# Adding partial sums in DRAM by the storing transfer, and letting ScalarE empty the accumulators

## The chip, the cores and the metric

The kernel runs on one core of a Trainium2 chip. The metric is device time in microseconds of one execution of the program. The median of three runs of the kernel before is 725.49 us (725.46 to 725.61).

## The reference

Attention over a small memory, then a gated feed-forward layer, all in float32, for 8 batches of 8 heads, 576 positions, head width 64:

```python
a = softmax(phi, over positions)                  # phi: (8, 8, 576, 32)
k_m, v_m = a^T k, a^T v                           # 32 memory rows per head
attn = softmax(q k_m^T / 8) v_m                   # (8, 8, 576, 64)
x = attn with heads side by side                  # (4608, 512)
out = (sigmoid(x w_gate) * (x w_val)) w_out       # d_ff = 1536
```

The output has 4608 rows of 512; each batch owns 576 of them.

## The kernel before

The hidden width of 1536 is cut into 12 tiles of 128, called f (0 to 11). A *step* is one batch with one f: TensorE makes gate and value (tiles `pu_t`) in two column halves c = 0 and 1 (`gate_half`), ScalarE takes the sigmoid (`sg`), VectorE the product, and the product is split in a high and a low part (`g_hi`, `g_lo`); then `out_half` multiplies it with the output weights into four accumulators in PSUM, `acc0` to `acc3`, one per 128 rows (t = 0 to 3) of the batch. Columns past 512 of two batches are gathered in `left` and done apart (`out_left`).

Batches 4 to 7 go through all 12 f at once. Batches 0 to 3 go in three rounds of four f (`turns`, L839): round one does f 0 to 3 for batches 0, 1, 2, 3, round two f 4 to 7, round three f 8 to 11. After each round a batch's accumulators have to leave, since the next batch uses the same four. That makes 48 steps, numbered 0 to 47; the first 12 are written out by hand (`OPENING`), the rest run in the loop at L1187, and after it (from L1352) batches 4 to 7 follow with an order of every engine written out by hand (`step`, `queued`: each instruction stands behind the last one of its engine).

In the loop, `out_half` lags: a finished f's half c = 0 is multiplied in the next step and its half c = 1 at the beginning of the one after (`pend`, `LAG` = 3). So for the last f of a round, tiles 0 and 1 leave in the step after and tiles 2 and 3 one step later. The next batch writes `acc0` and `acc1` again about one step after they left, and `acc2` and `acc3` likewise. The order of all TensorE instructions is that of the code (`in_turn`, L183). A scheduler orders the other engines' instructions of the loop; it follows the code's order where it can.

How a tile leaves is `leave` (L727). In round one it copies the accumulator into a tile called `row` (128 x 512; ScalarE for odd t, VectorE for even t), and GpSimd stores it into a DRAM tile `part`. In rounds two and three the earlier sum has been loaded from `part` into a `row` beforehand (`row_of`, L754, on SyncE's queue), VectorE adds accumulator and `row` (L732), and GpSimd stores the sum to a new `part` (round two) or to the output (round three). The loads are asked for one f ahead of the end (L722 to L725, and L1207 to L1209 for the last batch).

There are four rooms for `row` (`bufs=4`). A tile that asks for one waits until the transfer that read its last holder has landed. The rooms are also used by others: in steps 32 to 37 (L1197 to L1206) each step takes two of them for differences of the gate weights, made by VectorE at L1205 and stored by SyncE to the kept weights (`wgv`); late on, the left columns of batches 2 to 7 (`left_hi`, `left_lo`, L769) and the memories of batches 6 and 7 (L379, L413) take them.

Transfers are issued by `move` (L169) on two queues: "batch" is SyncE (SP), "stream" is GpSimd (POOL). On each, the transfers start in the order of the code. POOL has the stores of `row`, and in steps 12 to 30 the loads of weight words that are converted there. SP has everything else: loads of `row`, reloads of `at`, kept weights, inputs of the next batches. A transfer that reads what another one wrote waits for that one's landing, and the queue waits with it.

Of the kernel before, what the change touches and what calls it, by code (L numbers as in the profile page):

```python
# [9 lines left out]
F32 = mybir.dt.float32  # L10
# [3 lines left out]
ALU = mybir.AluOpType  # L14
# [3 lines left out]
P = 128  # L18
B, H, S, D, M = 8, 8, 576, 64, 32
DM, DFF = 512, 1536  # L20
NG = 2
NKT = 4
NFT = DFF // P
SF = 4
# [14 lines left out]
QUAD = 4  # L39
TURN = 4  # L40
# [58 lines left out]
def attn_moe_kernel(  # L99
# [10 lines left out]
    nc = tc.nc  # L110

    keep = ctx.enter_context(tc.tile_pool(name="keep", bufs=1))
    dram = ctx.enter_context(tc.tile_pool(name="dram", bufs=1, space=bass.MemoryType.DRAM))
    sb = ctx.enter_context(tc.tile_pool(name="att", bufs=1))
    mb = ctx.enter_context(tc.tile_pool(name="moe", bufs=1))
    early = ctx.enter_context(ExitStack())
    po = ctx.enter_context(tc.tile_pool(name="po", bufs=1, space=PSUM))
    banks = ctx.enter_context(ExitStack())
    pu = banks.enter_context(tc.tile_pool(name="pu", bufs=NB, space=PSUM))
    pools = {"conv": early.enter_context(tc.tile_pool(name="conv0", bufs=1))}  # L120
# [14 lines left out]
    def att(shape, name, bufs=1):  # L135
        return sb.tile(shape, F32, name=name, bufs=bufs)
# [11 lines left out]
    def wo_of(f):  # L148
        return [t[:, f % NE, :] for t in wos[f // NE]]
# [16 lines left out]
    queues = {"batch": nc.sync, "stream": nc.gpsimd}  # L166
    last_move = {}

    def move(dst, src, queue="batch"):  # L169


        with ExitStack() as behind:
            if queue in last_move:
                behind.enter_context(tc.issue_after(last_move[queue].ins))
            last_move[queue] = queues[queue].dma_start(dst, src)  # L175

    def rest(lo, x, hi):

# [12 lines left out]
    def matmul(*args, **kw):  # L191
        in_turn(nc.tensor.matmul, *args, **kw)
# [109 lines left out]
    def convert(f, k):  # L302
        to_f32(whole_of(f, k), f, k)
        if k == 2:
            wo_hi(f)
            wo_lo(f)
# [257 lines left out]
    def again(b):  # L564
        new_at(b)
        for d, a in zip(kept[b], at[b]):
            move(a.rearrange("p r n -> p (r n)").bitcast(F32), d)
# [4 lines left out]
    def make_u(b, fs):  # L572

        nf = len(fs)
        pb = [bank()[:, : nf * 256].rearrange("p (f x) -> p f x", f=nf) for _ in range(2)]
        for p in range(H):
            rs, l = of_head(b, 1, p)
            js = slice((p // 2) * M, (p // 2 + 1) * M)
            r = wg[rs, fs[0] : fs[0] + nf, ORDER[b % 2][p] // 2, :]
            matmul(pb[p % 2][js], l, r, start=True, stop=True)  # L580
        U[b, fs[0], "pb"] = pb
# [21 lines left out]
    def part_u(b, fs):  # L603
        for r in range(2):
            u_hi(b, r, *fs)
            u_lo(b, r, *fs)
# [12 lines left out]
    @contextmanager  # L619
    def behind():  # L620


        with ExitStack() as stack:
            for last in (last_act, last_prod, last_u, last_conv):
                stack.enter_context(tc.issue_after(last[0].ins))
            yield
# [3 lines left out]
    part = {}  # L630
# [68 lines left out]
    def gate_all(b, f, c):  # L699
        for do in (gate_half, sigmoid, product, g_hi, g_left, g_lo):  # L700
            do(b, f, c)

    def out_half(b, f, c, at_start, at_end, later=False):

        hi, lo = G.pop((b, f, c))
        w_hi, w_lo = wo_of(f)
        if lo is None:
            terms = [(hi, raws[f])]
        else:
            terms = [(hi, w_hi), (hi, w_lo), (lo, w_hi)]  # L710
        for j in range(2):
            t = 2 * c + j
            if at_start:
                acc[b, t] = po.tile([P, DM], F32, name=f"acc{t}")
            ts = slice(j * P, (j + 1) * P)
            for i, (l, r) in enumerate(terms):
                last = at_end and i == len(terms) - 1
                matmul(acc[b, t], l[:, ts], r, start=at_start and i == 0, stop=last)
        if at_end and not later:
            for j in range(2):  # L720
                leave(b, f, 2 * c + j)
        if (b, f + 1) in ends and c:  # L722
            for t in range(SF):
                if (b, t) in part and (b, t) not in rows:
                    rows[b, t] = row_of(b, t)  # L725

    def leave(b, f, t):  # L727

        o = acc.pop((b, t))
        st = last_rows(t) if b == B - 1 else rows.pop((b, t), None) or row_of(b, t)  # L730
        if (b, t) in part:
            nc.vector.tensor_tensor(st, o, st, op=ALU.add)  # L732
            part.pop((b, t))
        elif t % 2 or "banks" in pools:
            nc.scalar.copy(st, o)
        else:
            nc.vector.tensor_copy(st, o)
        if f == NFT - 1:
            queue = "batch" if b >= QUAD else "stream"
            move(out[b * S + t * P : b * S + (t + 1) * P, :], st, queue)  # L740
        else:
            part[b, t] = dram.tile([P, DM], F32, name=f"part{b}_{t}_{f}")
            move(part[b, t], st, "stream")

    rows = {}
    room_of_last = []

    def last_rows(t):

        if not room_of_last:  # L750
            room_of_last.append(att([P, SF, 512], "kvm0"))
        return room_of_last[0][:, t, :]

    def row_of(b, t):  # L754

        st = mb.tile([P, DM], F32, name="row", bufs=4)
        if (b, t) in part:
            move(st, part[b, t])
        return st

    def u_tiles():
        return [mb.tile([P, 2, 2, 256], F32R, name=f"u_{p}", bufs=2) for p in ("hi", "lo")]
# [41 lines left out]
    def run(*parts):  # L804
        for p in parts:
            for _ in p:
                pass
# [34 lines left out]
    ends = {(b, f) for b, f, _, at_end in steps if at_end}  # L842
# [157 lines left out]
    MAIN = begin[QUAD, 0]  # L1000
# [28 lines left out]
    def go_on():  # L1029

        nonlocal pieces, slots
        for _ in range(-(-pieces // max(slots, 1))):
            next(beside, None)
            pieces -= 1
        slots -= 1
# [8 lines left out]
    def load_pair(n):  # L1044

        if n >= NPAIRS:
            return
        in_ring[n] = lp[0].tile([P, 2, NKT, 256], F32, name="ring")
        move(in_ring[n].rearrange("p f k n -> p (f k n)"), kept_w[n % NP])
# [137 lines left out]
    for i, (b, f, at_start, at_end) in enumerate(steps[:MAIN]):  # L1187
        if i < LISTED:
            continue
        if i in sides:  # L1190
            run(beside)
            beside, pieces = chain(*(g for _, g in sides[i])), sum(n for n, _ in sides[i])
            length = next(n for n in range(i + 1, len(steps) + 1) if n == len(steps) or steps[n][2]) - i
            slots = 2 * length - 1 - sum(i <= n < i + length for n in quad_at)
        if i in returns:
            again(returns[i])
        k = i - begin[0, NFT - TURN]  # L1197
        if 0 <= k < NP:
            w, kept_k = wg[:, 2 * k : 2 * k + 2], kept_w[k].rearrange("p (f k n) -> p f k n", f=2, k=NKT)
            move(kept_k[D:], w[D:])  # L1200
            move(kept_k[:D, :, :, :P], w[:D, :, :, :P])
            for j in range(2):
                t = mb.tile([P, DM], F32, name="row", bufs=4)[:D]
                t = t.rearrange("p (k n) -> p k n", k=NKT)
                nc.vector.tensor_tensor(t, w[:D, j, :, :P], w[:D, j, :, P:], op=ALU.subtract)  # L1205
                move(kept_k[:D, j, :, P:], t)  # L1206
        if i == MAIN - 2:  # L1207
            for t in range(SF):
                rows[b, t] = row_of(b, t)  # L1209
        if i == MAIN - TURN:  # L1210
            weights.close()
            lp[0] = weights.enter_context(tc.tile_pool(name="late2", bufs=1, side="right", reuse_waits="tile"))
            load_pair(0)
        extra = out_left(*lefts[i]) if i in lefts else iter(())
        gate_all(b, f, 0)
        for job in CONVERT.get(i, ()):
            with behind():
                convert(*job)
        next(extra, None)
        if i in u_at:  # L1220
            if steps[i + 1][0] != b:
                run(beside)
            make_u(*u_at[i])
            part_u(*u_at[i])
        while len(pend) >= LAG:
            out_half(*pend.pop(0))
        pend.append((b, f, 0, at_start, at_end))
        go_on()
        gate_all(b, f, 1)
        while len(pend) >= LAG and i < MAIN - 1:  # L1230
            out_half(*pend.pop(0))
        if i in quad_at:
            quad(i)
        if i == MAIN - 2:
            pair_u(0, [bank(), bank()])
            for name in "rl":
                u_out(0, name)
            u_sums(0, 0, 1, 2)
            for name in "lrs":
                part_hi(0, name)  # L1240
                part_lo(0, name)
        pend.append((b, f, 1, at_start, at_end))
        next(extra, None)
        if i not in quad_at:
            go_on()
        del U[b, f]
# [283 lines left out]
```

## Time and profile before

| | |
|---|---|
| median of three runs | 725.49 us |
| the profiled execution | 725.69 us, its span 723.9 us |
| PE (TensorE) | busy 98% of the span |
| DVE (VectorE) | 74% |
| ACT (ScalarE) | 58% |
| POOL (GpSimd) | 5% |
| DMA | 124.64 MB, 172 GB/s in the mean |

PE is TensorE's matmul, PEld its weight load, SP is SyncE with its queue SPq. L189 is the line of the helper that records every matmul, L175 that of the helper that issues every transfer, so rows are told apart by their tiles. "Time to landing" of a transfer runs from its issue to its landing. The rounds lie as follows: round one ends at about 165 us, round two at about 270, round three at about 389; steps 36 to 38, the first three of batch 1 in the third round, run from about 287 to 306 us, six microseconds each.

### The profile page before, as it was taken

To read this page: it belongs to the slowest core of one execution; us is meant where nothing else is said; L and a number is where in the kernel's file an instruction comes from. 1 tells how busy PE (TensorE), PEld (TensorE's weight loads), DVE (VectorE), ACT (ScalarE), POOL (GpSimd) and SP (SyncE) were. 2 spreads that over 40 slices of the span, in tenths; PEclk is the share of its full clock that TensorE was granted. 3 is DMA by queue.
4 is the path that set the end of the run, shared out by engine and by line. 5 is a ranking of instruction groups with operands and counts; after the bars stand their busy time and mean duration, and the time that the engine had idled before them with its cause. 6 is when DMAs were issued, how large, how long until landed. Compare 5 with 4: busy or idle time off the path is not lost.

```text
span 723.9 us, 14181 instructions
## 1 busy us (share of the span) xinstructions
PE 710.5 (98%) x5524; PEld 583.4 (81%) x5524; DVE 535.6 (74%) x1048; ACT 423.0 (58%) x984; POOL 36.3 (5%) x71
## 2 busy tenths in 40 slices
PE   8899999999999999999999999999999999999997
PEld 6656778888888988988878877887788788888786
DVE  5999998767777855567549678776787768977663
ACT  4676775454444433336455676875777657686553
POOL 0000100111102110110101000000000000000000
PEclk9999999999999999999999999999999999999999
DMA  8994629649457549871557113652323422141102
GB/s 349 420 389 141 253 83 379 238 137 363 136 191 264 175 158 225 305 247 33 160 216 275 59 59 114 226 182 68 109 73 114 146 94 78 59 175 60 59 1 73
DMA packets 37907, 124.64 MB, mean 172 GB/s; under 512 B 4241, under 2 KB 11665, under 8 KB 31697
## 3 DMA queue, kind: packets, MB, share of 16 engines
q1 hardware_dynamic: 31744, 103.04, 40.3%
q0 software_dynamic: 6096, 20.71, 8.1%
q8 instruction: 43, 0.70, 0.4%
q14 instruction: 24, 0.19, 0.1%
HBM read 94.90 MB, written 28.84 MB: 171 GB/s over the span
## 4 chain that ended last, share of the span: by engine, by line
PE 87%; DVE 6%; ACT 3%; DMA 2%; issue 1%; SPq 0%; DVEq 0%; ACTq 0%
PE acc L189 36%; PE pu_t L189 25%; PE c L189 8%; PE a L189 8%; PE b L189 5%; PE d L189 5%; DMA kvm<-in_kvm_dram 2%; ACT ph L164 1%; DVE e L484 1%; DVE e L501 1%; DVE zs L497 1%; DVE mx L482 1%; DVE e L475 1%; DMA q<-in_qT_dram 0%; SPq L175 0%
## 5 line engine op out<-in xcount | busy, mean ns | idle before, releaser
L189 PE MATMUL pu_t<-at,u_hi 128*128 128x320 f32 (+1 forms) x752 | 156.2, 303 | 0.2 <-DVE sg L672 0.2
L189 PE MATMUL acc<-wo_hi,g_hi 128*128 128x512 f32 x372 | 151.2, 406 | 0.0
L189 PE MATMUL acc<-wo_hi,g_lo 128*128 128x512 f32 x372 | 146.8, 395 | 0.0
L189 PE MATMUL acc<-wo_lo,g_hi 128*128 128x512 f32 x372 | 146.5, 394 | 0.0
L189 PEld LDWEIGHTS pu_t<-at,u_hi 128*128 128x128 f32 x752 | 124.2, 188 | 11.8 <-issue 3.0
L189 PE MATMUL pu_t<-at,u_lo 128*128 128x320 f32 (+1 forms) x360 | 106.3, 295 | 0.0
L189 PEld LDWEIGHTS acc<-wo_hi,g_hi 128*128 128x128 f32 x372 | 69.8, 188 | 34.2 <-issue 11.7
L189 PEld LDWEIGHTS acc<-wo_hi,g_lo 128*128 128x128 f32 x372 | 69.9, 188 | 17.1 <-DVE g_lo L179 0.8
L164 ACT ACTIVATE sg<-pu_t 128x256 f32<-128x256 f32 (+1 forms) x94 | 38.6, 411 | 75.8 <-PE pu_t L189 75.7
L189 PEld LDWEIGHTS acc<-wo_lo,g_hi 128*128 128x128 f32 x372 | 70.0, 188 | 6.3
L672 DVE TENSOR_TENSOR sg<-pu_t,sg 128x256 f32<-128x256 f32 (+1 forms) x92 | 41.5, 454 | 42.8 <-ACT sg L164 29.9
L682 ACT CAST g_hi<-sg 128x256 fp32r<-128x256 f32 x90 | 36.4, 406 | 54.5 <-DVE sg L672 53.3
L189 PEld LDWEIGHTS pu_t<-at,u_lo 128*128 128x128 f32 x360 | 67.8, 188 | 0.0
L1155 ACT COPY c_p<-c 128x288 f32<-128x288 f32 x48 | 19.2, 400 | 53.3 <-PE c L189 52.8
L179 DVE TENSOR_TENSOR g_lo<-sg,g_hi 128x256 fp32r<-128x256 f32 x90 | 37.4, 419 | 11.0 <-ACT g_hi L682 11.0
L1159 DVE TENSOR_TENSOR z<-c,c_x 128x288 f32<-128x288 f32 x48 | 21.9, 456 | 31.8 <-PE c L189 28.6
L164 ACT ACTIVATE z<-z 128x288 f32<-128x288 f32 x96 | 37.9, 438 | 7.5 <-DVE z L1159 7.4
L1171 ACT CAST g_hi<-z 128x512 fp32r<-128x512 f32 x48 | 29.9, 622 | 17.7 <-DVE z L1166 17.7
L1159 DVE TENSOR_TENSOR z<-a,c_s 128x288 f32<-128x288 f32 x48 | 21.7, 452 | 24.4 <-PE a L189 22.8
L179 DVE TENSOR_TENSOR u_lo<-pu_t,u_hi 128x512 fp32r<-128x512 f32 (+1 forms) x46 | 28.6, 672 | 10.5 <-ACT u_hi L595 10.5
L179 DVE TENSOR_TENSOR g_lo<-z,g_hi 128x512 fp32r<-128x512 f32 x48 | 32.8, 683 | 1.2 <-ACT g_hi L1171 1.2
L595 ACT CAST u_hi<-pu_t 128x512 fp32r<-128x512 f32 (+1 forms) x46 | 24.0, 587 | 13.8 <-PE pu_t L189 13.6
(246 smaller groups left out, 1473.1 us busy)
## 6 DMA issues: line engine op xcount, KB each, us to landing
ring<-wgv SPq DMA_DIRECT2D x24, 1024.0 KB, 4.8
at<-at SPq DMA_DIRECT2D x24, 576.0 KB, 6.8
kvm<-in_kvm_dram SPq DMA_DIRECT2D x12, 1024.0 KB, 10.2
q<-in_qT_dram SPq DMA_DIRECT2D x16, 512.0 KB, 4.7
part<-row POOLq DMA_DIRECT2D x32, 256.0 KB, 4.9
row<-part SPq DMA_DIRECT2D x32, 256.0 KB, 4.0
wg<-in_kvm_dram SPq DMA_DIRECT2D x4, 1024.0 KB, 11.8
out_dram<-row POOLq DMA_DIRECT2D x16, 256.0 KB, 5.1
```

The lines of the kernel that those rows point to most:

```text
L164: last_act[0] = nc.scalar.activation(*args, **kw)
L179: return nc.vector.tensor_tensor(lo, x, hi.bitcast(F32), op=ALU.subtract)
L189: last_pe[0] = do(*args, **kw)
L475: nc.vector.transpose(blocks(b, c)[:, r].rearrange("p w m -> p (w m)"), t)
L482: nc.vector.tensor_reduce(mx, e, axis=AX.X, op=ALU.max)
L484: nc.vector.tensor_tensor(e, e, mx.unsqueeze(3).broadcast_to([P, 2, w, M]), op=ALU.subtract)
L595: nc.scalar.copy(hi[:, r, :nf], U[b, fs[0], "pb"][r])
L672: last_prod[0] = nc.vector.tensor_tensor(prod, ps[1][:, :n], sg[:, :n], op=ALU.mult)
L682: nc.scalar.copy(hi, prod[:, : 2 * P])
L1155: nc.scalar.copy(getattr(self, name), self.c if name == "p5" else self.d)
L1159: nc.vector.tensor_tensor(self.z[:, i], x, y, op=ALU.add)
L1171: nc.scalar.copy(self.g[0], self.z[:, 2:4, : 2 * P])
```

## The change

In rounds two and three nothing is loaded any more. ScalarE copies the accumulator into a `row` for all four tiles (before, VectorE added there), and GpSimd's storing transfer adds it in DRAM to the batch's `part` (`accum_op=ALU.add`). There is one `part` per tile for all three rounds. In the third round GpSimd then issues a second transfer that copies the finished `part` from DRAM to the output. A `row` is asked for when the tile leaves. Round one and batches 4 to 7 are as before.

```diff
--- before.py
+++ after.py
@@ -166,13 +166,13 @@
     queues = {"batch": nc.sync, "stream": nc.gpsimd}
     last_move = {}
 
-    def move(dst, src, queue="batch"):
+    def move(dst, src, queue="batch", **kw):
 
 
         with ExitStack() as behind:
             if queue in last_move:
                 behind.enter_context(tc.issue_after(last_move[queue].ins))
-            last_move[queue] = queues[queue].dma_start(dst, src)
+            last_move[queue] = queues[queue].dma_start(dst, src, **kw)
 
     def rest(lo, x, hi):
 
@@ -719,30 +719,26 @@
         if at_end and not later:
             for j in range(2):
                 leave(b, f, 2 * c + j)
-        if (b, f + 1) in ends and c:
-            for t in range(SF):
-                if (b, t) in part and (b, t) not in rows:
-                    rows[b, t] = row_of(b, t)
 
     def leave(b, f, t):
 
         o = acc.pop((b, t))
-        st = last_rows(t) if b == B - 1 else rows.pop((b, t), None) or row_of(b, t)
-        if (b, t) in part:
-            nc.vector.tensor_tensor(st, o, st, op=ALU.add)
-            part.pop((b, t))
-        elif t % 2 or "banks" in pools:
+        st = last_rows(t) if b == B - 1 else row_of()
+        if t % 2 or f >= TURN:
             nc.scalar.copy(st, o)
         else:
             nc.vector.tensor_copy(st, o)
-        if f == NFT - 1:
-            queue = "batch" if b >= QUAD else "stream"
-            move(out[b * S + t * P : b * S + (t + 1) * P, :], st, queue)
+        to = out[b * S + t * P : b * S + (t + 1) * P, :]
+        if b >= QUAD:
+            move(to, st)
+        elif f < TURN:
+            part[b, t] = dram.tile([P, DM], F32, name=f"part{b}_{t}")
+            move(part[b, t], st, "stream")
         else:
-            part[b, t] = dram.tile([P, DM], F32, name=f"part{b}_{t}_{f}")
-            move(part[b, t], st, "stream")
-
-    rows = {}
+            move(part[b, t], st, "stream", accum_op=ALU.add)
+            if f == NFT - 1:
+                move(to, part.pop((b, t)), "stream")
+
     room_of_last = []
 
     def last_rows(t):
@@ -751,12 +747,8 @@
             room_of_last.append(att([P, SF, 512], "kvm0"))
         return room_of_last[0][:, t, :]
 
-    def row_of(b, t):
-
-        st = mb.tile([P, DM], F32, name="row", bufs=4)
-        if (b, t) in part:
-            move(st, part[b, t])
-        return st
+    def row_of():
+        return mb.tile([P, DM], F32, name="row", bufs=4)
 
     def u_tiles():
         return [mb.tile([P, 2, 2, 256], F32R, name=f"u_{p}", bufs=2) for p in ("hi", "lo")]
@@ -1204,9 +1196,6 @@
                 t = t.rearrange("p (k n) -> p k n", k=NKT)
                 nc.vector.tensor_tensor(t, w[:D, j, :, :P], w[:D, j, :, P:], op=ALU.subtract)
                 move(kept_k[:D, j, :, P:], t)
-        if i == MAIN - 2:
-            for t in range(SF):
-                rows[b, t] = row_of(b, t)
         if i == MAIN - TURN:
             weights.close()
             lp[0] = weights.enter_context(tc.tile_pool(name="late2", bufs=1, side="right", reuse_waits="tile"))
```

## Rows read from the trace of the kernel before

**Rows 1.** The page's part 1: busy time, share of the span and instructions of each engine
```profile
PE 710.5 (98%) x5524; PEld 583.4 (81%) x5524; DVE 535.6 (74%) x1048; ACT 423.0 (58%) x984; POOL 36.3 (5%) x71
```

**Rows 2.** Busy time per stretch: length, PE, PEld, DVE, ACT, POOL, granted clock, DMA share, GB/s
```profile
0.00:90.00 90.00, 81.99 (x924) 59.04 (x925) 76.66 (x129) 58.74 (x127) 2.45 (x9) 1.00 0.80 310
90.00:165.00 75.00, 75.00 (x536) 62.83 (x535) 61.08 (x116) 44.23 (x102) 10.85 (x20) 1.00 0.59 214
165.00:265.00 100.00, 100.00 (x750) 85.15 (x749) 71.38 (x147) 45.88 (x114) 11.04 (x20) 1.00 0.63 218
265.00:310.00 45.00, 45.00 (x290) 39.34 (x288) 26.95 (x55) 14.64 (x41) 4.32 (x8) 1.00 0.85 247
310.00:410.00 100.00, 100.00 (x836) 82.13 (x836) 68.03 (x132) 53.29 (x122) 7.59 (x14) 1.00 0.49 172
410.00:700.00 290.00, 288.72 (x2083) 237.81 (x2082) 222.57 (x458) 197.56 (x462) 0.00 (x0) 1.00 0.29 101
700.00:724.00 24.00, 19.83 (x114) 17.14 (x112) 8.93 (x18) 8.64 (x20) 0.00 (x0) 0.97 0.16 56
```

**Rows 3.** Instructions on tile row: count, shortest/median/longest ns, first and last start
```profile
L175 POOL DMA_DIRECT2D part<-row x32: 539/542/682, 80.4 to 270.2; - x32
...
L175 SPq DMA_DIRECT2D row<-part x32: 319/320/832, 169.4 to 362.3; - x32
...
L732 DVE TENSOR_TENSOR row<-acc,row x32: 672/681/692, 188.6 to 388.2; 128x512 f32<-128x512 f32 x32
...
L735 ACT COPY row<-acc x20: 560/588/607, 78.5 to 647.1; 128x512 f32<-128x512 f32 x20
```

**Rows 4.** Waits of SP's queue: total us, times, longest
```profile
SPq L175 <- DMA part<-row: 61.2, 12, 17.3
```

**Rows 5.** Timeline of DVE: start, us, instruction, idle time before it and its releaser
```profile
272.50 0.68 DVE L1205 TENSOR_TENSOR row<-wg 64x512 f32<-64x512 f32 x1 [0.67 <-DMA part<-row]
...
291.89 1.52 DVE L732 TENSOR_TENSOR row<-acc,row 128x512 f32<-128x512 f32 x2
...
299.11 0.68 DVE L1205 TENSOR_TENSOR row<-wg 64x512 f32<-64x512 f32 x1 [2.94 <-DMA out_dram<-row]
```

**Rows 6.** Timeline of PE, accumulator matmuls from 291 to 301 us
```profile
291.19 0.39 PE L189 MATMUL acc<-wo_hi,g_lo 128*128 128x512 f32 x1
...
299.52 0.39 PE L189 MATMUL acc<-wo_hi,g_hi 128*128 128x512 f32 x1
...
300.22 0.39 PE L189 MATMUL acc<-wo_hi,g_hi 128*128 128x512 f32 x1
```

**Rows 7.** Timeline of ACT around batch 0's leave
```profile
290.71 0.40 ACT L682 CAST g_hi<-sg 128x256 fp32r<-128x256 f32 x1
...
292.00 0.41 ACT L682 CAST g_hi<-sg 128x256 fp32r<-128x256 f32 x1 [0.89 <-DVE sg L672]
```

**Rows 8.** Timeline of POOL, stores of batches 0 and 1 in the third round
```profile
292.86 0.54 POOL L175 DMA_DIRECT2D out_dram<-row  x1 [22.13 <-DVE row L732]
...
318.57 1.22 POOL L175 DMA_DIRECT2D out_dram<-row  x2 [21.90 <-DVE row L732]
```

**Rows 9.** Tile row on POOL, 290 to 300 us: time to landing of its four stores
```profile
DMA to landing us min/median/max: 5.2/5.7/6.3
```

**Rows 10.** Tile row on POOL, 264 to 273 us: time to landing of its four stores
```profile
DMA to landing us min/median/max: 2.3/2.8/3.0
```

**Rows 11.** Tile part on SP, 270 to 290 us: time to landing of its four loads
```profile
DMA to landing us min/median/max: 3.0/5.1/5.2
```

**Rows 12.** Transfers by issue, POOL: count, KB each, median us to landing
```profile
part<-row POOLq DMA_DIRECT2D x32, 256.0 KB, 4.9
...
q<-in_wgv_dram POOLq DMA_DIRECT2D x6, 512.0 KB, 5.1
```

**Rows 13.** Tile left_hi on ACT, 400 to 430 us: first and last start
```profile
L774 ACT CAST left_hi<-left x2: 622/624/625, 405.1 to 421.7; 128x512 fp32r<-128x512 f32 x2
```

## The prediction

> **What bounds the kernel now.** I read the busy times first. TensorE (PE) is busy for 710.5 of 723.9 us, VectorE (DVE) for 74% and ScalarE (ACT) for 58% [rows 1]. A share over the whole span hides stages, so the table by stretch comes next [rows 2]: from 90 to 410 us PE is busy for every microsecond, at the full clock, 2.4 GHz; from 410 to 700 us it idles for 1.28 us in all; the rest of its idle time lies before 90 us (8.0) and after 700 us (4.2). The change touches nothing before about 160 us (the partial sums of the first round leave as before) and nothing after batch 3 has left. So all that it can save is the idle time of PE from 90 to 700 us, 1.28 us or 0.18%. An error in the other direction has no such ceiling: any microsecond for which PE waits is added to the end. The question is therefore which late thing reaches PE. I call 0.2% (1.45 us) what a measurement of this kernel can tell from no change.
>
> **The change part by part.** The profiled execution took 725.69 us, 1.8 more than its span; it stands 0.20 above the median of the three runs (725.49), so I add to 725.69 and take off 0.2 at the end.
>
> *Removed:* 32 adds of DVE, 681 ns each, 21.8 us [rows 3], and 32 loads by SP, about 320 ns of its queue each. PE waited for neither between 90 and 410 us [rows 2], so this frees time that nobody on the path was waiting for: 0. *Added on ACT:* 32 copies of 588 ns [rows 3], 18.8 us. 28 of them fall where ACT is 33 to 53% busy [rows 2]; the cover is PE's own queue of ready work, and I take 0. The last four, of batch 3 (383 to 389 us), fall in the order written out by hand; they cost 0 if ACT's waits for PE take them in, and 4 x 0.59 = 2.4 us if none does. I take 0, since PE has no idle time there either.
>
> *Added on POOL:* 16 more transfers of 0.54 us of issue [rows 3], 8.7 us on an engine that is 5% busy. The issue time is free; the order is not. For each of the 16 finished tiles POOL now issues the adding store, then must wait until it has landed before it issues the copy to the output, and only then comes to the adding store of the next tile. That a transfer which reads what another wrote waits for the landing, and holds its whole queue meanwhile, is what SP's row loads do in the trace before: 12 waits, 61.2 us in all [rows 4]. Behind each wait on POOL stands the next tile's adding store, and who waits for that store is whoever wants its "row" room again. Before the change nothing in POOL's queue waited for a landing of its own.
>
> *Moved:* the four "row" rooms. Before, a room is taken early, for the load; now a tile takes one as it leaves. In the second round each store is sent at once and each room is back one landing later, so nothing is late. In the third round the place to look at is batch 0, because there the same four rooms also serve the kept weight pieces, two per step in steps 32 to 37. By the order in which the code asks, the eight requests are: two pieces (step 36), tiles 0 and 1, two pieces (step 37), tiles 2 and 3. In the trace before, rooms go round in the order of asking: the first piece of step 33 (272.50 us) waited for a store of batch 3, by its time that of tile 2, which had asked four places earlier, and the first of step 36 (299.11) for an output store of batch 0 [rows 5]. So I read it that tile 2 now gets the room of tile 0 and tile 3 that of tile 1, whose adding store stands on POOL behind tile 0's landing.
>
> *The sum.* PE's last matmul into tile 0 begins at 291.19 and takes 0.39 [rows 6]; ACT is free from 291.1 to 292.0 [rows 7]; the copy ends at 292.2. POOL's store began 0.3 us after the DVE add of tile 0 ended (291.89 + 0.68, against 292.86) [rows 5, 8], so the first adding store is issued at 292.5. Call its time to landing T. Copy to the output: 0.54. Second adding store: T. Tile 3's copy out of the accumulator: 0.59. PE may then write tile 3's accumulator for batch 1, at 292.5 + 2T + 1.13; before it did so at 300.22 [rows 6]. Tile 2 needs only one T and is due at 299.52. The stall is 2T - 6.6 us, and PE, full up to the end of the stage, never makes it good.
>
> *T* is the unknown; no row shows an adding store. The same 256 KB stored plainly took 5.2 to 6.3 us to land in this stretch, median 5.7 [rows 9], and 2.3 to 3.0 at 267 to 270 us, where less was moving [rows 10]. Below 2.3 I see no reason to go, since the bytes are the same and one more read is added. From above: the store plus a whole load of the tile, whose rows here have median 5.1 [rows 11], 10.8 us. Between these ends the nearest row is the same store in the same stretch, with what twice the bytes cost on POOL's queue: 512 KB land in 5.1 us where 256 KB take 4.9 [rows 12], so 0.2 more. I take T = 5.9. Stall: 2 x 5.9 - 6.6 = 5.2 us. With T = 2.3 it is none; with 10.8 it is 15.0 us.
>
> The Trainium skill ("DMA: Bandwidth & Descriptors", section "Anatomy of one DMA — SWDGE (gpsimd) path") fits such a transfer as 2.0 us plus its bytes at 436 GB/s; as an estimate for 512 KB read and written that gives 3.2 us, and by it the stall would be gone. The rows of 267 to 270 us are near it, those of this stretch are not (5.7 where the fit has 2.6).
>
> *Elsewhere in the third round* I cost the chain at nothing: four tiles take 4 x (5.9 + 1.08) = 28 us on POOL, and the next batch's stores began 25.7 us later (292.86 and 318.57 [rows 8]), the shortest gap of the three; that batch's first rooms were last used by tiles 0 and 1 and by the pieces, and are long back. After batch 3 the rooms are next asked for by the left columns at 405.1 us [rows 13]: its first two tiles, stored from 383.7 us, are then back for any T up to about 10.
>
> Sum: 725.69 + 5.2 = 730.9 for the profiled time, 730.7 against the median.
>
> **The rivals.**
> *No stall.* T is short, or the rooms go round otherwise (tiles 2 and 3 get those of the pieces of step 36, stored by SP and back by about 297). It decides at 2T < 6.6, T < 3.3 us. For it: the 2.3 to 3.0 us at 267 to 270 us, and SP's loads no longer share the DMA engines just before. Against it: DMA engines are 85% busy from 265 to 310 us [rows 2]. Its time is that of before, 725.5, since nothing else reaches PE. Chance 0.36. The skill's fit would make this the outcome.
> *Backlog.* T near its upper end, from 9 us on: the chain of four takes 40 us and more, the stall is 11.4 us at T = 9 and 15.0 at 10.8, and the left columns start to wait at 405 us. 737 to 741 us. Against it: no row of a 256 KB store in this stretch is above 6.3. Chance 0.07.
> *Faster.* DVE's 21.8 us or SP's freed queue close the gaps of PE after 410 us: at best all 1.28 us, 724.2. Against it: those gaps are small, and batches 4 to 7 are unchanged. Chance 0.05, with some of the scatter of a new schedule.
> *The change doing nothing* is no rival by itself: accumulating stores replace loads in any case; that they have no effect on time is the first one.
>
> **How the numbers follow.** The forecast, a stall at batch 0's third round of 2 to 11 us, has 0.52; with the backlog, slower has 0.59. No stall and stalls under 1.45 us (T below 4.0) are "same", 0.36; faster 0.05. The likeliest time is 730.7; the forecast's own range is 727.5 to 737. The range over all cases reaches down to the no-stall time, 725.2, and up to T = 9, 737; the backlog and most of the faster case stay out, with a few per cent of scatter.
>
> **What would show it.** Right: PE idle at about 299.5 to 305 us in front of an accumulator matmul, put down to ACT's copy out of it; that copy waiting on the landing of a transfer from "row"; POOL's waits headed by landings of the adding store, 16 of them; PE busy throughout elsewhere up to 410 us; time to landing of the adding stores near 6 us. DVE's busy time down by 22 us and ACT's up by 19 with no effect show the first parts. Wrong: PE gapless at 300 us although the landings are over 4 us (then the rooms, step "Moved", are wrong), landings under 3.3 us (then T), or a longer time with PE waiting elsewhere, above all for ACT in 380 to 410 us.

## The result, and the profile after

The changed kernel takes 729.37 us (median of 4 runs, 728.32 to 730.37) against 725.49 before: 1.0051 times as long, with an interval of 1.0038 to 1.0063. That is 3.9 us slower, where 5.2 were forecast. Measured again later it took 727.98 us (6 runs, 726.73 to 730.14) against 725.62 for the kernel before on that chip, 1.0040 [1.0026, 1.0054]. The size moves from run to run within 2 to 3.5 us. The runs of the kernel before lay within 0.15 us beside the first measurement and within 0.7 beside the second; beside the experiments below they reach up to 1.6 us. Three runs of the whole record that took 1155 us and more, two of the kernel before and one of plain_store, are left out. The profiled execution took 729.30 us, its span is 727.5.

The page's part 1, after; it answers to [rows 1]:

```profile
PE 711.2 (98%) x5524; PEld 583.5 (80%) x5524; DVE 518.0 (71%) x1016; ACT 437.0 (60%) x1016; POOL 56.5 (8%) x87
```

VectorE has 32 instructions fewer and 17.6 us less, ScalarE 32 more and 14.0 us more, POOL 16 more and 20.2 us more. None of it is a gain. The table by stretch, with the columns of [rows 2]:

```profile
165.00:265.00 100.00, 100.00 (x751) 85.13 (x750) 66.42 (x137) 50.88 (x126) 15.69 (x20) 1.00 0.64 178
265.00:310.00 45.00, 44.04 (x279) 37.66 (x278) 20.68 (x43) 17.24 (x46) 7.18 (x9) 1.00 0.89 221
310.00:410.00 100.00, 98.44 (x803) 81.22 (x802) 58.17 (x112) 57.20 (x130) 19.73 (x28) 1.00 0.63 172
410.00:700.00 290.00, 288.73 (x2110) 237.32 (x2109) 223.80 (x463) 198.56 (x465) 0.51 (x1) 1.00 0.30 104
```

PE had no idle time from 265 to 410 us before; it now has 0.96 and 1.56 us. TensorE's instructions come in the same order in both kernels, so the loss can be placed more closely: I set the start of each matmul beside that of the same matmul before. It runs later by

| place in the kernel before | what | later by |
|---|---|---|
| 274.25 us | batch 3's accumulators, second round | 1.03 us, 1.14 from the next matmul on |
| 281 to 285.5 us | gate halves, next `u` | 1.55 us |
| 299.52 us | batch 0's accumulators, third round | 2.02 us, 2.13 from the next matmul on |
| 377.32 us | matmuls on `ring`, a load of SP | 3.76 us |
| the end | | 3.71 us |

TensorE (PE), timeline after; columns: start, length, instruction, idle time before it and its releaser. These are the first matmuls of the three places that show idle time:

```profile
275.28 0.51 PE L189 MATMUL acc<-wo_hi,g_hi 128*128 128x512 f32 x1 [0.57 <-ACT row L728]
...
301.54 0.50 PE L189 MATMUL acc<-wo_hi,g_hi 128*128 128x512 f32 x1 [0.31 <-ACT row L728]
...
381.08 0.59 PE L189 MATMUL c<-ring,vT 64*32 64x512 f32 x1 [1.56 <-DMA ring<-wgv]
```

In the kernel before, the second of these stands in [rows 6]; the first and the third are, without idle time,

```profile
274.25 0.39 PE L189 MATMUL acc<-wo_hi,g_hi 128*128 128x512 f32 x1
...
377.32 0.61 PE L189 MATMUL c<-ring,vT 64*32 64x512 f32 x1
```

ACT's copies out of the accumulators, the same timeline for that engine; it shows what stood behind the first two:

```profile
265.64 0.59 ACT L728 COPY row<-acc 128x512 f32<-128x512 f32 x1 [0.79 <-PE acc L189]
...
266.57 0.58 ACT L728 COPY row<-acc 128x512 f32<-128x512 f32 x1
...
273.11 0.59 ACT L728 COPY row<-acc 128x512 f32<-128x512 f32 x1 [4.01 <-DMA part<-row]
274.64 0.58 ACT L728 COPY row<-acc 128x512 f32<-128x512 f32 x1 [0.95 <-DMA wgv<-row]
...
293.18 0.59 ACT L728 COPY row<-acc 128x512 f32<-128x512 f32 x1 [0.79 <-PE acc L189]
...
294.12 0.59 ACT L728 COPY row<-acc 128x512 f32<-128x512 f32 x1
...
300.90 1.07 ACT L728 COPY row<-acc 128x512 f32<-128x512 f32 x2 [4.26 <-DMA part<-row]
```

Both times tiles 0 and 1 leave at once; tile 2 waits for the landing of an adding store (`part<-row`), and tile 3 follows 0.5 to 1.5 us behind. At 274.64 it is released by the store of a kept piece (`wgv<-row`). POOL's timeline:

```profile
266.52 1.80 POOL L175 DMA_DIRECT2D part<-row  x2 [20.00 <-ACT g_hi L682]
...
294.06 0.86 POOL L175 DMA_DIRECT2D part<-row  x1 [17.68 <-ACT row L728]
301.37 0.54 POOL L175 DMA_DIRECT2D out_dram<-part  x1 [6.45 <-DMA part<-row]
301.89 0.92 POOL L175 DMA_DIRECT2D part<-row  x1
306.68 0.53 POOL L175 DMA_DIRECT2D out_dram<-part  x1 [3.87 <-DMA part<-row]
```

The store at 294.06 landed after 6.7 us, at 300.8: tile 2's copy starts at 300.90. Tile 1's adding store is issued only at 301.89, when tile 3's copy is already under way. So tile 3 didn't wait for tile 1's room. The store of a kept piece, issued by SP at 293.87, landed at 301.19, and tile 3's copy began at 301.39. The pieces, in VectorE's timeline:

```profile
247.96 0.68 DVE L1197 TENSOR_TENSOR row<-wg 64x512 f32<-64x512 f32 x1 [2.15 <-DMA part<-row]
...
265.93 1.29 DVE L1197 TENSOR_TENSOR row<-wg 64x512 f32<-64x512 f32 x2 [0.21 <-DMA wgv<-row]
274.98 1.28 DVE L1197 TENSOR_TENSOR row<-wg 64x512 f32<-64x512 f32 x2 [5.43 <-DMA wgv<-row]
...
293.17 0.67 DVE L1197 TENSOR_TENSOR row<-wg 64x512 f32<-64x512 f32 x1
```

Two pieces are written just as tiles 0 and 1 take two rooms, at 265.93 and again at 293.17 (the second of that pair follows at 293.8). With that all four rooms are held, until a transfer lands.

The rooms cost time in a second way, too. In VectorE's order the gate's products (`sg`) stand behind pieces, and a piece that waits for a room holds them up. VectorE after, and the same product before:

```profile
280.93 0.68 DVE L1197 TENSOR_TENSOR row<-wg 64x512 f32<-64x512 f32 x1 [1.92 <-DMA wgv<-row]
281.54 0.41 DVE L672 TENSOR_TENSOR sg<-pu_t,sg 128x256 f32<-128x256 f32 x1
```

```profile
275.25 0.41 DVE L672 TENSOR_TENSOR sg<-pu_t,sg 128x256 f32<-128x256 f32 x1
```

The product is 6.3 us late where TensorE is 1.2, and those behind it catch up only in part: the one of 282.95 us comes at 286.02, and the matmuls of the second row of the table wait for it.

**Theory:** the loss comes from the "row" rooms, which leaving tiles share with the kept pieces; the adding store holds a room longer than the plain one did (6.5 and 7.3 us for the two at 266.52, against 2.3 to 3.0 in [rows 10]). **Rivals:** POOL's chain of store, landing and copy to the output delays the next store, as the prediction had it; ScalarE's copies are late in themselves; the `ring` load. "Slip" below means how much later the same matmul starts than in the kernel before. Diffs are against the changed kernel, where nothing else is said.

### The profile page after: what moved, and what is told of

It reads as the page before. It is cut to its first block, busy times and chain, and to the rows that moved or that the text cites. A ratio compares the mean times of both kernels' runs of the same rounds, so it can differ in the third digit from the quotient of the medians.

```text
span 727.5 us, 14125 instructions
## 1 busy us (share of the span) xinstructions
PE 711.2 (98%) x5524; PEld 583.5 (80%) x5524; DVE 518.0 (71%) x1016; ACT 437.0 (60%) x1016; POOL 56.5 (8%) x87
## 4 chain that ended last, share of the span: by engine, by line
PE 82%; DVE 6%; DMA 6%; ACT 3%; issue 1%; SPq 0%; ACTq 0%; DVEq 0%
PE acc L189 34%; PE pu_t L189 22%; PE c L189 8%; PE a L189 8%; PE b L189 5%; PE d L189 5%; DMA wgv<-row 2%; DMA kvm<-in_kvm_dram 2%; DMA ring<-wgv 1%; DMA part<-row 1%; ACT ph L164 1%; DVE e L484 1%; DVE e L501 1%; DVE zs L497 1%; DVE mx L482 1%
## 5 line engine op out<-in xcount | busy, mean ns | idle before, releaser
L175 POOL DMA_DIRECT2D part<-row x48 | 38.3, 871 | 185.9 <-DVE row L730 82.9
L728 ACT COPY row<-acc 128x512 f32<-128x512 f32 x52 | 30.1, 590 | 15.9 <-DMA part<-row 8.3
```

What stands on the lines that cost most here:

```text
L175: last_move[queue] = queues[queue].dma_start(dst, src, **kw)
```

## The experiments

**POOL's chain taken away (into_out).** The first store and the adding ones go straight into the output rows, so POOL waits for no landing and copies nothing.

```diff
-            part[b, t] = dram.tile([P, DM], F32, name=f"part{b}_{t}")
+            part[b, t] = to
...
-            if f == NFT - 1:
-                move(to, part.pop((b, t)), "stream")
```

> The first store of a batch's tile goes to its rows of the output and both later rounds add there, so the 16 copies from DRAM to the output and POOL's 16 waits for a landing are gone; the rooms are shared as before. Theory 1 (TensorE lost 1.5 us at 273 to 287 us and 0.5 us at 300 us because tile 2's copy waits for a row room until tile 0's adding store has landed, and 1.7 us at 377 us because the ring load lies beside POOL's chain of adding stores and copies of batch 2): the 1.7 us go, the room waits stay: 727.6 us (727.0 to 728.2). Theory 2 (the chain of waits on POOL is what holds the rooms, as in the prediction): the wait at 300 us goes too, and with it 0.5 us more. Theory 3 (ScalarE's 32 copies are the cost): no change, 729.4.

Measured: 730.31 us (729.11 to 732.85), 1.0069 [1.0055, 1.0084], no faster than the change itself, where 727.6 was expected. The wait for `ring` is gone (its load lands after 4.7 us), but the accumulators wait longer. ACT's copies of tiles 2 and 3 in its timeline:

```profile
301.49 0.59 ACT L728 COPY row<-acc 128x512 f32<-128x512 f32 x1 [5.14 <-DMA out_dram<-row]
...
303.32 0.59 ACT L728 COPY row<-acc 128x512 f32<-128x512 f32 x1 [1.25 <-DMA wgv<-row]
```

The adding stores of tiles 0 and 1 now start together, at 293.77 and 294.7, and land after 7.6 and 8.3 us (in the change the first one took 6.7). Tile 3 is released by a piece's store here too. The slip is 1.27 us at 285 and 3.74 at 300 us. So taking the chain away doesn't give the time back.

**The chain kept, but out of the way (copies_last).** Four adding stores first, then the four copies to the output.

```diff
-            if f == NFT - 1:
-                move(to, part.pop((b, t)), "stream")
+            if f == NFT - 1 and t == SF - 1:
+                for u in range(SF):
+                    move(out[b * S + u * P : b * S + (u + 1) * P, :], part.pop((b, u)), "stream")
```

> In the third round POOL issues a batch's four adding stores one behind the other and its four copies to the output after them, so no adding store waits behind another's landing. Theory 1: rooms wait for a single landing in any case, so the stalls at 273 and 300 us stay; batch 2's transfers are through by about 368 us, before the ring load is issued at 372.6, so the ring wait goes: 727.6 us (727 to 728.3). If the ring load is late for another reason: 729.4. Theory 2 (the chain on POOL holds the rooms): the stall at 300 us goes as well, 727.1.

Measured: 730.55 us (729.32 to 731.69), 1.0066 [1.0054, 1.0078]. Missed in the same way. Two stores issued at 293.90 and 294.8 land after 8.4 and 8.8 us; PE's timeline at batch 0:

```profile
302.99 0.50 PE L189 MATMUL acc<-wo_hi,g_hi 128*128 128x512 f32 x1 [1.93 <-ACT row L728]
...
304.73 0.50 PE L189 MATMUL acc<-wo_hi,g_hi 128*128 128x512 f32 x1 [0.77 <-ACT row L728]
```

The two waits make 2.7 us, and the clock fell after them (last section). In both runs the first store landed later than in the change, with a second one 0.9 us behind it. That the second one made it late is not shown: the last section has a profile that speaks against it.

**The same store without its sum (plain_store).**

```diff
-            move(part[b, t], st, "stream", accum_op=ALU.add)
+            move(part[b, t], st, "stream")
```

> The stores of rounds two and three overwrite in place of adding, so the sums over f are left out of the output; every instruction, room and wait is otherwise that of the changed kernel. Theory 1 (rooms come back late because an adding store takes longer to land than a plain one, 6 to 7 us against 3 at 267 us): the stall at 273 us goes, that at 300 us shrinks to nothing, and the ring wait shrinks: 726.0 to 727.3 us. Theory 2 (only the serial chain on POOL counts): little change at 273 us, 728.5 to 729. Theory 3 (ScalarE's copies): no change, 729.4.

Measured: 726.04 us (725.25 to 726.94), 1.0004 [0.9995, 1.0013]; the sums over f are left out of the output, and chain, copies and rooms are all as in the change. The store at 266.65 lands after 4.1 us, tile 2 is copied at 270.83 and PE loses nothing there; the one at 292.59 lands after 6.6 us, and PE loses 0.4 us at 300. What a store that adds costs over a plain one is thus most of the loss, and the profiles place it mainly at batch 3: the first store there took 4.2 to 7.0 us in the eleven profiles in which it adds, 2.3 to 4.1 in the three in which it is plain. At batch 0 the plain one took as long here (6.6 us) as the adding one in the change (6.7). POOL's issue of it is shorter too: 539 ns against 862.

**The pieces out of the rooms (pieces_aside, aside_into, before_aside).** The differences of steps 32 to 35 are written over the gate weights that they are made from, which are not read again; the two steps that need a room move to 38 and 39. In pieces_aside this is the only edit, aside_into has the edit of into_out as well, and before_aside is the kernel before with this edit alone, as a control.

```diff
+        k = k if k < 4 else k - 2 if k > 5 else -1
...
-                t = mb.tile([P, DM], F32, name="row", bufs=4)[:D]
-                t = t.rearrange("p (k n) -> p k n", k=NKT)
+                if k < 4:
+                    t = w[:D, j, :, P:]
+                else:
+                    t = mb.tile([P, DM], F32, name="row", bufs=4)[:D]
+                    t = t.rearrange("p (k n) -> p k n", k=NKT)
```

> The differences for the kept weights of steps 32 to 35 are written over the gate weights themselves (no longer read there), those of steps 36 and 37 are made in steps 38 and 39, so that no piece holds a row room when batch 3's second round and batch 0's third round leave. Theory 1: tiles 2 and 3 find free rooms, ScalarE no longer waits for a landing at 269 to 273 and 297 to 301 us, and 1.5 + 0.5 us come back: 727.4 us (726.8 to 728), with the ring wait left. Theory 3 (ScalarE's copies cost the time, whatever room they get): 729.4.

> Both earlier edits together: no kept piece holds a row room when tiles leave, and the rounds add directly in the output, so POOL issues no copies and waits for no landing. Theory 1 (room waits at 273 to 300 us, and the ring load at about 371 us sharing the DMA engines with batch 2's chain of adding stores and copies): both are gone, 725.5 us (725.2 to 725.9), and no run near 727.3 as three of the eleven with the pieces aside alone. If those slower runs have nothing to do with POOL's chain, they stay.

> The kernel before, with only the edit of the pieces (four pairs written over the gate weights, two made two steps later). It is the control for that edit. TensorE did not wait in that stretch, so theory 1 expects no change: 725.6 us (725.3 to 725.9). If it were clearly faster, the recovery with the pieces aside would not be the rooms'.

Measured: pieces_aside 725.65 us (725.28 to 727.36, 11 runs), 1.0006 [0.9997, 1.0015]; aside_into 725.65 (725.38 to 727.13), 0.9999 [0.9990, 1.0008]; before_aside 725.74 (725.50 to 726.13), 0.9998 [0.9989, 1.0006]. The edit gives the kernel before nothing and gives the changed one all that it had lost; its last slip is -0.02 us. That is more than was expected: the wait for `ring` is gone as well, with a load that landed after 5.7 us. Three of the eleven runs of pieces_aside stand at 727.2 to 727.4 us, one of aside_into at 727.13, where none was expected, and one of the kernel before beside it at 727.16. None of these has a profile; what they lose stays open. ACT's copies in pieces_aside:

```profile
265.64 0.59 ACT L728 COPY row<-acc 128x512 f32<-128x512 f32 x1 [0.79 <-PE acc L189]
...
266.58 0.59 ACT L728 COPY row<-acc 128x512 f32<-128x512 f32 x1
...
268.45 0.59 ACT L728 COPY row<-acc 128x512 f32<-128x512 f32 x1 [0.25 <-PE acc L189]
269.24 0.59 ACT L728 COPY row<-acc 128x512 f32<-128x512 f32 x1
...
294.40 0.59 ACT L728 COPY row<-acc 128x512 f32<-128x512 f32 x1 [0.26 <-PE acc L189]
295.19 0.59 ACT L728 COPY row<-acc 128x512 f32<-128x512 f32 x1
```

No copy waits for a landing any more; the matmuls release them. The landings themselves are no shorter: the first stores at batch 3 and at batch 0 took 6.8 and 6.1 us, in the change 6.5 and 6.7. And POOL's waits in the same run, beside those of the change: the first row is pieces_aside,

```profile
POOL out_dram L175 <- DMA part<-row: 80.9, 16, 8.0
```

and this one the change:

```profile
POOL out_dram L175 <- DMA part<-row: 80.6, 16, 8.6
```

The chain of POOL is untouched and costs nothing here: in this profile the stores' landings mattered only through the rooms.

**Either half of it (early_aside, late_aside).** early_aside keeps the pieces of steps 32 to 35 out of the rooms, late_aside moves only those of steps 36 and 37. In early_aside:

```diff
-                t = mb.tile([P, DM], F32, name="row", bufs=4)[:D]
-                t = t.rearrange("p (k n) -> p k n", k=NKT)
+                if k < 4:
+                    t = w[:D, j, :, P:]
+                else:
+                    t = mb.tile([P, DM], F32, name="row", bufs=4)[:D]
+                    t = t.rearrange("p (k n) -> p k n", k=NKT)
```

and, in late_aside,

```diff
+        k = k if k < 4 else k - 2 if k > 5 else -1
```

> Only the pieces of steps 32 to 35 are written over the gate weights; those of steps 36 and 37 keep their row rooms at the place where batch 0's third round leaves. Theory 1: the stall of batch 3's second round (1.15 us at 273 us and 0.35 at 285 us) goes; at 300 us tile 2 has to wait only if the pieces of step 36 and 37 and tiles 0 and 1 fill the four rooms, which they do: 0.5 to 2 us stay. 726 to 727.7 us.

> Only the pieces of steps 36 and 37 move to steps 38 and 39; those of steps 32 to 35 keep their rooms. Theory 1: the stall at 273 to 287 us stays (1.2 to 2 us), that at 300 us goes since four rooms are free for batch 0's tiles: 726.8 to 728 us, plus up to 1.7 when the ring load is late.

> The kernel with only the early pieces aside once more, for a second profile: its runs lay between 726.3 and 731.3 us, and the one profile was of the fastest. Theory 1: the rest lies at 300 us (tile 2 waiting for tile 0's adding store, longer when that lands later, and the granted clock lower behind a long wait) or at the ring load at 371 us, nowhere else; median 727.5 to 729.

Measured: early_aside 728.58 us (726.30 to 731.27), 1.0041 [1.0025, 1.0057], above what was expected; late_aside 727.59 (726.82 to 729.38), 1.0032 [1.0020, 1.0044], as expected. The same kernel once more (early_again): 727.37 (726.85 to 728.77), 1.0025 [1.0015, 1.0036], just under the 727.5 to 729 expected. The profiles separate the two places. In early_aside tiles 2 and 3 of batch 3 leave at 268.59 and 269.38 unhindered, and the one wait is at batch 0, which adds 0.62 us of slip in its first profile and 1.59 in the second. First early_aside, then early_again:

```profile
299.59 1.08 ACT L728 COPY row<-acc 128x512 f32<-128x512 f32 x2 [4.42 <-DMA part<-row]
```

```profile
300.66 1.07 ACT L728 COPY row<-acc 128x512 f32<-128x512 f32 x2 [5.38 <-DMA part<-row]
```

In late_aside it is the other way about: the one wait for a landing is at batch 3, and batch 0's tiles 2 and 3 leave at 295.69 and 296.48 without one.

```profile
270.81 1.07 ACT L728 COPY row<-acc 128x512 f32<-128x512 f32 x2 [1.67 <-DMA part<-row]
```

Its slip, 1.30 us, appears by 281 us in front of gate matmuls, by way of VectorE, and stays. So the early pieces make the loss at batch 3, and the late ones that at batch 0. Runs of early_aside above 729 have no profile; why they are so long stays open.

**Three rooms instead of four (three_rooms).** Every `name="row", bufs=4` or `tag="row", bufs=4` becomes `bufs=3`:

```diff
-        return mb.tile([P, DM], F32, name="row", bufs=4)
+        return mb.tile([P, DM], F32, name="row", bufs=3)
```

> The changed kernel with three row rooms in place of four. Theory 1: now tile 3 of every batch waits for tile 0's adding store, and with the pieces of steps 32 to 37 in the same three rooms the stalls at 273 and 300 us grow to several us each: 732 to 742 us. If rooms are not what TensorE waits for: 729 to 730.

Measured: 741.50 us (740.57 to 744.28), 1.0227 [1.0210, 1.0245]. The slip is 12.9 us by 302 us and 15.0 at the end; ACT's copies wait for both kinds of holder, stores of tiles and stores of pieces:

```profile
ACT row L728 <- DMA part<-row: 13.9, 8, 2.8
...
ACT row L728 <- DMA wgv<-row: 7.5, 3, 3.1
```

Some of it (2.0 us by 115 us) lies in the opening, before anything is added, about 1.5 us is a lower clock behind the longest wait (last section), and 1.8 us, at 390.6 us of the kernel before, lies in front of a matmul that ScalarE releases with other work. Most of the rest is the same waits, enlarged: copies out of accumulators, and gate products held up on VectorE.

**ScalarE let off (dve_leave).** VectorE makes the copies of rounds two and three.

```diff
-        if t % 2 or f >= TURN:
+        if b < QUAD and f >= TURN:
+            nc.vector.tensor_copy(st, o)
+        elif t % 2 or f >= TURN:
```

> The changed kernel with VectorE instead of ScalarE emptying the accumulators in rounds two and three. Theory 1: whichever engine copies waits for the same row rooms and holds what is behind it, 728 to 731 us. Theory 3 (the move to ScalarE costs the time): 725.5 to 726.

Measured: 728.50 us (727.68 to 729.48), 1.0035 [1.0022, 1.0047], the slip in the same places (1.3 us by 285, 2.6 at 299.5 us). VectorE's copy of tile 2 waits 4.95 us for `part<-row`, as ScalarE's did. Which engine copies makes no difference that these runs show.

**The change once more (after_again).**

> The changed kernel itself once more, beside the two halves of the edit on the same chip: 728.3 to 730.4 us as before, with the stalls at 273, 285 and 300 us in the profile. Whether the ring load is late again is open: theory 1 expects it late when an adding store of batch 2 is issued within a microsecond of it, and in time otherwise.

Measured: 727.98 us (726.73 to 730.14), 1.0040 [1.0026, 1.0054], a little under what was expected. In its profile (726.89 us) the slip is 0.88 us by 286, 1.29 at 300 and 1.31 at the end. The room waits are there, smaller: batch 3's accumulators lose nothing, and the 0.9 us lie in front of gate matmuls that wait for VectorE. PE doesn't wait for `ring` at all. Its load was issued at 371.9 us and landed after 5.6 us. In the first profile it was issued at 372.6, 0.5 us behind an adding store on POOL (372.12), and landed after 8.3; before it took 4.7. Only that one profile shows this wait. That the adding store just ahead made the load late is not borne out: in after_again such a store stood 0.05 us ahead of it (371.88), in three_rooms 0.5 us. In the seven profiles other than the first in which an adding store stands 0.05 to 1.4 us ahead, the load took 5.6 to 6.6 us; where none does (into_out, copies_last, aside_into), 4.7 to 4.8. So what made it 8.3 stays open.

## Why the prediction was right and wrong

The time was forecast on the right side and 1.3 us too high. The way to it was in large part another.

**What held.** PE was full, so the 32 adds and 32 loads that went saved nothing. ScalarE's 32 copies cost nothing: pieces_aside, with them, is as fast as before, dve_leave, without them, lies between the two measurements of the change, and the last four, in the order written out by hand, add no slip. POOL's added issue was put at 8.7 us and came to 20.2, because an adding store takes longer to issue; pieces_aside has it too and loses nothing by it. T, the time to landing of an adding store, was taken as 5.9 us; the one it was used for took 6.7, all of them 4.2 to 9.0. The nearest row, the plain store in the same stretch [rows 9], was the right choice. The 3.2 us estimated from the fit in the Trainium skill ("DMA: Bandwidth & Descriptors", section "Anatomy of one DMA — SWDGE (gpsimd) path") are half the measured time. And the first stall that was named, an accumulator matmul at 300 us that waits for a copy, which waits for a landing, is there.

**Step "Moved" failed.** It gave tile 2 the room of tile 0 and tile 3 that of tile 1, and so put two landings in a row on the path: 2T - 6.6. The first half holds (landing at 300.8, copy at 300.90). The second doesn't: tile 3 got the room of a piece and came right behind tile 2. One landing remains. The first store was issued when forecast (294.06 is 292.5 plus the 1.55 us by which PE was late by then), and with 6.7 us it made 0.47 us of slip (0.6 with the next matmul), not 5.2. The rival "No stall" had the rooms of tiles 2 and 3 both go to those of the pieces; the truth lies between.

**POOL's chain** was the reason given for the second landing. Its 16 waits came as forecast (80.6 us in all), but pieces_aside, with 80.9 us of the same waits, is as fast as before, and the two runs without waits between the adding stores, into_out and copies_last, are no faster than the change.

**The second round, costed at nothing,** lost the larger part of what the rooms cost: 1.03 us at batch 3, and 0.5 more by 285.5 us, part of it by way of VectorE, whose pieces wait for rooms with the gate's products behind them. The prediction has no term for that way. The sentence "each store is sent at once and each room is back one landing later, so nothing is late" left out that the pieces of steps 32 to 35 already hold rooms there, VectorE having made the first ones as early as 247.96 us, and that the tiles used to take their rooms an f before they left. The trace before showed it [rows 5]: the piece at 272.50 waited for a store of batch 3, so the two met already. The prediction used that row for batch 0 and not for batch 3. Nor was the landing there short any more: 6.5 us, where [rows 10] had 2.3 to 3.0.

**"PE busy throughout elsewhere up to 410 us"** was wrong once more: 1.63 us of the profiled 3.7 are the `ring` load. Without it the profile would stand at about 727.7 us, near the second measurement. So the forecast was near the median by luck: a stall that was too large made up for these two that were missing.

**Cause.** Shown by pieces_aside against its control: the adding stores hold "row" rooms that the kept pieces also want, and where four holders meet, a copy out of an accumulator, or VectorE with the gate's work, waits for a landing. This accounts for the waits at 273 to 300 us. The wait for `ring` came in one profile of the change and is not explained. No kernel tried here is faster than the one before: with the pieces aside the change stands at 725.65 us, the same as before within the interval, since PE is full either way.

## What to carry to other kernels

Where one engine is full, work taken off the others buys nothing, and every new dependence is a chance to lose. In these runs the time also varied more once buffers came back with a landing: by 2 to 3.5 us, against 0.15 to 1.6 for the kernel before. A store that adds replaces a load made early by a buffer held late: count how long the buffer is held, with the store's landing as measured in that stretch. And list everyone who takes buffers from that ring, at the times at which the scheduler really runs them, not at the steps in which the code asks.

## What was not expected of the hardware

- An adding store of 256 KB takes POOL 0.86 to 0.93 us to issue in the stretches above, and up to 2.03 at the longest, against 0.54 for a plain one. Its time to landing scatters: the first one at batch 0 took 4.3 to 7.9 us in the eight profiles in which the next one waits for it. With a second one 0.9 us behind it, it took 7.6 us in into_out and 8.4 in copies_last, but 4.8 in aside_into, where no kept piece is stored at that time. So a second adding store close behind doesn't always make the first one late; what else did in those two is not shown.
- The granted clock fell after PE's waits in copies_last, from full speed (2.4 GHz) towards 1.2 GHz: table by stretch, columns as in [rows 2],

```profile
296.00:300.00 4.00, 4.00 (x26) 3.66 (x25) 0.46 (x2) 0.41 (x1) 0.00 (x0) 1.00 0.95 198
300.00:304.00 4.00, 2.04 (x13) 1.35 (x11) 0.00 (x0) 0.59 (x1) 0.77 (x1) 1.00 0.64 136
304.00:308.00 4.00, 3.27 (x12) 3.09 (x13) 1.77 (x4) 2.54 (x7) 2.35 (x5) 0.66 0.86 92
308.00:312.00 4.00, 4.00 (x25) 3.69 (x24) 0.92 (x2) 0.71 (x4) 0.60 (x2) 0.91 0.93 302
```

PE had waited 1.93 and 0.77 us just before. From 305.3 us on its matmuls take longer (those of 128x320 follow each other after 0.27 us, before after 0.15), until 308.6; with PE busy all the while the slip grows from 4.62 us at 305.30 to 6.15 at 308.83. So the lower clock cost 1.5 us on top of the waits. In three_rooms it fell as well, to 0.63 between 312 and 316 us, behind a single wait at the same batch, and the slip grew by 1.7 us by 315 us:

```profile
311.51 0.79 PE L189 MATMUL acc<-wo_hi,g_hi 128*128 128x512 f32 x1 [2.82 <-ACT row L728]
```

After waits of 1.18 and 0.86 us in into_out, and of 1.43 in early_again, at the same batch, the granted clock stayed at 1.00. So in these profiles waits that were 0.7 us longer in sum (2.70 against 2.04) were followed by 1.5 us more.
